# An mLSTM and mixer kernel: the weight decoding of the first batch moved back by one chunk

## The chip, the cores and the metric

The kernel runs on one core of a Trainium2 chip. The metric is the device time of one execution in microseconds (us). An execution's own time holds its span, which is what the profile shows, and a little around it.

## The reference

For four batches the kernel computes an mLSTM layer with 8 heads of 40 over 768 steps, and then a token and channel mixer with ReLU and residuals:

```python
for t in range(S):                      # mLSTM, kept stable by a running maximum m
    m_new = max(f_gate + m, i_gate)
    C = exp(f_gate + m - m_new) * C + exp(i_gate - m_new) * outer(v, k)
    n = exp(f_gate + m - m_new) * n + exp(i_gate - m_new) * k
    y = sigmoid(o_gate) * (C @ q) / max(abs(n @ q), 1)
x = y as [B, S, 320]
h = relu(x.T @ w_tok1) @ w_tok2         # over the tokens, 768 -> 256 -> 768
u = x + h.T
out = u + relu(u @ w_ch1) @ w_ch2       # over the channels, 320 -> 1536 -> 320
```

## The kernel before

**Work.** A batch's 768 steps are cut into NC = 6 chunks of 128. A chunk (a unit `(b, c)`) is done in matrix form: scores `ps_sc` from queries and keys (`st_s`, L313), times decays `dd` (L323), applied to the values into `po` (`st_pv`, L439) on top of the part from the state, which needs scaled queries `q3t` (`prep_q3`, L274 to L280; L378), and an update of the state (`st_state`, L386, L391, L395). `x0_ops` makes the chunk's output `x` from `po` (L476 to L485) and splits it into a high part `xh` on ScalarE (L490) and a low part `xl` (L491), since the mixer works with pairs of rounded fp32 numbers. The mixer over the tokens is `a_part` (matmuls `ps_a`, one row of products per chunk), `a_end` (Relu into `rh` on ScalarE, L711, and its low part `rl` on VectorE, L712), and `phase_b` (matmuls `ps_b` with `w2` from `rh` and `rl`). Both run through the helper `mm3`, L694. The mixer over the channels is `gemm1w` (L807) and `gemm2w`.

**Weights.** They come packed, in 30 pieces of 128 x 384: pieces 0 to 3 are `w1` (for ps_a), 4 to 7 `w2` (for ps_b), 8 and 9 the first of `c1`, 10 and 11 the first of `c2`, 12 and 13 `c1` again, and so on. A piece goes through five steps, in pairs:

- `dec_load` (L641): SyncE loads it into `wst`, up to the piece that the argument names.
- `dec_abs`: ScalarE makes `pf` in PSUM (L652, Prelu); then the lower bits are turned into integers in `wst`, by ScalarE (L656) or GpSimd (L658). While `early[0]` is set, ScalarE does this for every piece, and `pf` lies in the banks of `ps_acc`; later GpSimd does it for the even pieces, and `pf` lies in `ps_s`, unless a bank is named.
- `dec_ops`: VectorE joins both into `wf` (L670). This is a generator; each `step` runs one piece.
- `dec_hi`: ScalarE rounds `wf` into the high weights (L682).
- `dec_low`: GpSimd makes the low weights (L688).

**Order.** Each engine and the queue of SyncE serve their instructions in the order in which the program writes them; nothing is reordered. In the first batch a loop over c = 1 to 5 (L932 on) writes a turn: scores of the next chunk, its queries and keys, the state and output of this chunk, and the preparation of the chunk after. Into every turn it puts decoding. In turns 2 to 4 the two L670 of a pair stand between the halves of L323 (`mid=dg`) and behind the state update, in turn 1 both behind the state update. Behind the turn's output come `dec_hi`, `dec_low` and the next pair's `dec_abs`. In turn 4 pieces 8 and 9 are started in the middle, 10 at the end, and 11 at the end of turn 5. Behind the loop VectorE joins 8 and 9, TensorE finishes ps_a, and `rh`, `rl`, the transposes `gt` of the gates (L156, L158) and ps_b follow.

Of the kernel before, what the change touches and what calls it, by code (L numbers as in the profile page):

```python
# [19 lines left out]
NC = S // L  # L20
# [15 lines left out]
def kernel(ctx: ExitStack, tc: tile.TileContext, gates, qk, q3, kv, og,  # L36
# [7 lines left out]
    ps_acc = ctx.enter_context(tc.tile_pool(name="ps_acc", bufs=2, space=PSUM))  # L44
# [3 lines left out]
    def f32(x):  # L48
        return x.bitcast(F32)
# [175 lines left out]
    def load_qk(u, hf):  # L225
        b, c = u
        t = T.setdefault(u, {})
        if hf == 0:
            t["raw"] = raws[units.index(u) % 3]
        nc.sync.dma_start(out=t["raw"][64 * hf:64 * hf + D], in_=qk[b, c, hf])  # L230

    def load_phi(u):
        b, c = u
        T.setdefault(u, {})
        third = b < 2 and c % 3 == 2
        dd = ap.tile([128, H, L], F32, tag="p12" if third else "dd", name="dd", bufs=1 if third else 2)
        if b:
            nc.sync.dma_start(out=dd, in_=phi_d[c, b * HP:b * HP + H].partition_broadcast(128))
        T[u]["dd"] = dd

    def load_kv(u):
        b, c = u
        if b == 0 and c == 2:
            kvt = sp.tile([128, DM + H * E1], F32, tag="kv", name="kvt")
        else:
            kvt = ap.tile([128, DM + H * E1], F32, tag="kv", name="kvt")
        nc.sync.dma_start(out=kvt, in_=kv[b, c * L:(c + 1) * L, :])
        T[u]["kv"] = kvt
# [58 lines left out]
    def st_s(u, mult=True, mid=iter(()), rows=64, pool=(ps_s, "s")):  # L307
        t = T[u]
        t["s"] = [pool[0].tile([128, 4, L], F32, tag=pool[1], name="ps_sc") for _ in range(2)]
        for h in range(4):  # L310
            for hf in range(2):
                r = t["raw"][64 * hf:64 * hf + rows]
                nc.tensor.matmul(t["s"][hf][:, h, :], r[:, 1, h, :], r[:, 0, h, :], start=True, stop=True)  # L313
        if mult:
            st_p(u, mid)

    def st_p(u, mid=iter(())):
        t = T[u]
        for hf in range(2):
            if hf:  # L320
                next(mid, None)
            dd = t["dd"][:, 4 * hf:4 * hf + 4, :]
            nc.vector.tensor_tensor(dd, t["s"][hf], dd, ALU.mult)  # L323
# [148 lines left out]
    def x0_ops(u):  # L472
        b, c = u
        v = nc.vector
        po, n = T[u]["po"], T[u]["bank"][:, 400:400 + H]
        v.tensor_tensor(po[:, :, 0:D], po[:, :, 0:D],  # L476
                        sig[(b, c // 3)][:, c % 3, :].rearrange("p (h d) -> p h d", d=D), ALU.mult)
        yield
        den = ap.tile([128, H], F32, tag="den", name="den")
        v.tensor_scalar(den, po[:, :, D], 1.0, None, op0=ALU.max)  # L480
        v.scalar_tensor_tensor(n, po[:, :, D], -1.0, den, op0=ALU.mult, op1=ALU.max)
        v.reciprocal(den, n)
        yield
        x = ap.tile([128, DM], F32, tag="x", name="x", bufs=6)
        v.tensor_tensor(x.rearrange("p (h d) -> p h d", d=D), po[:, :, 0:D],  # L485
                        den.unsqueeze(2).to_broadcast([128, H, D]), ALU.mult)
        yield
        pool = xpool[2] if c in (3, 4) else sp
        xh, xl = (pool.tile([128, DM], F32R, tag=a, name=a, bufs=3 if pool is sp else 2) for a in ("xh", "xl"))
        nc.scalar.activation(xh, x, AF.Copy)  # L490
        (v if c == NC - 1 else nc.gpsimd).tensor_tensor(xl, x, f32(xh), ALU.subtract)  # L491
        xs[u] = (x, xh, xl)
        del T[u]
        yield
# [137 lines left out]
    nxt = [0, 0, 0]  # L632
    his, lows, wx, early = [], [], [], [True]

    def dec_load(n):
        while nxt[0] < min(n, len(pieces)):
            d, w, a = pieces[nxt[0]]
            k = nxt[0]
            pool, n_b = (xpool[2], 2) if k in (2, 3, 8, 9) else (wx[0], 3) if wx and (k - wx[1]) % 7 < 3 else (wq, 4)
            t = pool.tile([128, WP, 2], I32, tag="wst", name="wst", bufs=n_b)  # L640
            nc.sync.dma_start(out=t.rearrange("p n t -> p (n t)"), in_=w[:, a:a + WP].bitcast(I32))  # L641
            staged[nxt[0]] = t
            nxt[0] += 1
# [3 lines left out]
    def dec_abs(n, bank=None, both=False):  # L647
        while nxt[1] < min(n, len(pieces)):
            raw = staged[nxt[1]]
            pool, tag = bank or ((ps_acc, "acc") if early[0] else (ps_s, "s"))  # L650
            f = pool.tile([128, WP], F32, tag=tag, name="pf")
            nc.scalar.activation(f, raw[:, :, 1].bitcast(F32), AF.Prelu, scale=W_BIAS, alpha=W_SIGN)  # L652
            low = raw[:, :, 0]
            top16 = raw.rearrange("p n t -> p (n t)").bitcast(U16).rearrange("p (n t) -> p n t", t=4)[:, :, 1]
            if early[0] or nxt[1] % 2 and not both:
                nc.scalar.activation(low, top16, AF.Identity, scale=2.0 ** -13, bias=floor_b)  # L656
            else:
                nc.gpsimd.tensor_scalar(low, top16, 2.0 ** -13, 2.0 ** -14 - 0.5, op0=ALU.mult, op1=ALU.add)  # L658
            ready[nxt[1]] = (f, wq.tile([128, WP], F32, tag="wf", name="wf", bufs=4))
            nxt[1] += 1  # L660

    def dec_ops(more, m=2):
        n = nxt[2]
        if n >= len(pieces):
            return
        v = nc.vector
        ps = [(staged.pop(m),) + ready.pop(m) + pieces[m] for m in range(n, min(n + m, len(pieces)))]
        for p in ps:
            raw, f, w, *_ = p
            v.scalar_tensor_tensor(w.bitcast(I32), f.bitcast(I32), 3, raw[:, :, 0],  # L670
                                   op0=ALU.logical_shift_left, op1=ALU.bitwise_or)
            his.append(p)
            yield
        nxt[2] += len(ps)
        if more:
            dec_load(n + more)
        yield

    def dec_hi(n=2):
        for _ in range(min(n, len(his))):  # L680
            _, _, f, d, _, a = his.pop(0)
            nc.scalar.activation(d[0][:, a:a + WP], f, AF.Copy)  # L682
            lows.append((f, d, a))

    def dec_low(n=4):
        for _ in range(min(n, len(lows))):
            f, d, a = lows.pop(0)
            nc.gpsimd.tensor_tensor(d[1][:, a:a + WP], f, f32(d[0][:, a:a + WP]), ALU.subtract)  # L688
# [86 lines left out]
    acc = {}  # L775
# [71 lines left out]
    def step(g, n=1):  # L847
        for _ in range(n):
            next(g, None)
# [61 lines left out]
    x0 = x0_ops(u0)  # L911
# [18 lines left out]

    for c in range(1, NC):
        u, n1, n2, n3 = (units[c + i] for i in range(4))  # L932
        if c == 1:
            st_s(n1)
        elif c < NC - 1:
            dg = dec_ops(0)
            st_s(n1, mid=dg)
        if c < 3:
            load_phi(n3)
            load_qk(n3, 0)  # L940
            load_qk(n3, 1)
        if c == 1:
            dec_load(4)
        if c < NC - 1:
            spread_q(n1)
            prep_q3(n1)
            prep_kw(n1)
        if c == NC - 2:
            rows_w()
            early[0] = False  # L950
            dec_abs(nxt[1] + 2)
        if c == 1:
            dec_abs(2)
        st_state(u)
        if c == 1:
            dg = dec_ops(0)
        if c < NC - 1:
            step(dg, 2 if c == 1 else 9)
        st_pv(u)
        if c < 4:  # L960
            load_kv(n2)
            load_q3(n2)
        dec_load(2 * c + 4)
        x0 = x0_ops(u)
        step(x0, 2)
        if c == 2:
            nc.sync.dma_start(out=phi_d.rearrange("c r t -> r c t"), in_=phi.rearrange("p (c t) -> p c t", t=L))
        if c < 4:
            spread_split(n2)
            prep_exp(n2, 0)  # L970
            prep_exp(n2, 1)
        if c == NC - 2:
            a_part(0, 0, 0)
            a_part(0, 1, 0)
        if c < NC - 1:
            step(dg, 9)
            dec_hi()
            dec_low()
            if c == NC - 2:
                step(x0, 9)  # L980
                dec_abs(nxt[1] + 1, (ps_acc, "acc"))
            else:
                dec_abs(nxt[1] + 2)
        step(x0, 9)
        if c == NC - 1:
            dec_abs(nxt[1] + 1, (ps_acc, "acc"))
        if c > 3:
            load_sig(1, c - 4)
    ss = (ps_s, "s")
    dg = dec_ops(0)  # L990
# [9 lines left out]
    for b in range(B):  # L1000
# [35 lines left out]
        if b == 0:  # L1036
# [9 lines left out]
            dg = dec_ops(9)  # L1046
# [128 lines left out]
```

## Time and profile before

| | before |
|---|---|
| median of 3 runs | 426.87 us (426.71 to 427.46) |
| the profiled execution | 426.81 us, of which the span is 424.9 us |
| TensorE busy | 419.7 us (99%) |
| VectorE, ScalarE, GpSimd busy | 280.5, 184.0, 142.7 us |
| chain that ended last | TensorE 94% |
| granted TensorE clock in the span | 1.0 of full speed |

Times in the profile are microseconds from the start of the span. A busy TensorE is not TensorE at its peak, since its matmuls overlap; where an instruction starts, and for what it waited, is read from the timeline of its engine. In a timeline several equal instructions stand in one line (x2), with the time from the first's start to the last's end; neighbours on one engine overlap a little, so the distance from one start to the next is shorter than the duration.

### The profile page before, as it was taken

Reading aid. Unit: us, or ns where it says so; the run is one execution under the profiler, and the core shown is the slowest. Engines: PE = TensorE matmul, PEld = TensorE weight load, DVE = VectorE, ACT = ScalarE, POOL = GpSimd, SP = SyncE. Lnnn points to the kernel's source line nnn. Section 1 sums busy time; section 2 is a strip of 40 time slices with the busy share of each in tenths; the row PEclk is TensorE's granted clock in tenths of the full one; section 3 lists DMA queues with packets and bytes.
Section 4 is the critical chain, followed back from the end, with each engine's and each line's share of the span. In section 5 each row is a group of like instructions: output and inputs, shape, how many; then the busy total and the mean of one; then the engine's idle time right before and its main releaser. Section 6 shows DMA issues by size and latency. Waiting matters only on the chain.

```text
span 424.9 us, 8988 instructions
## 1 busy us (share of the span) xinstructions
PE 419.7 (99%) x3510; PEld 396.8 (93%) x3510; DVE 280.5 (66%) x620; ACT 184.0 (43%) x426; POOL 142.7 (34%) x186
## 2 busy tenths in 40 slices
PE   8999999999999999999999999999999999999996
PEld 4888989999999999999999999999999999988996
DVE  8988565515876788799696698789796647111412
ACT  5978569893455635234323346334144112111211
POOL 7488488751544501241341230331350110000000
PEclk9999999999999999999999999999999999999999
DMA  7997658941876713333346121533320000000000
GB/s 218 278 292 268 241 170 290 272 147 52 253 199 195 213 39 104 123 117 125 95 154 195 35 93 43 137 116 93 119 86 32 0 23 12 0 2 0 35 28 31
DMA packets 24574, 52.34 MB, mean 123 GB/s; under 512 B 2565, under 2 KB 13325, under 8 KB 24533
## 3 DMA queue, kind: packets, MB, share of 16 engines
q1 hardware_dynamic: 24293, 51.61, 39.4%
q8 instruction: 27, 0.44, 0.5%
q10 hardware_dynamic: 240, 0.18, 0.1%
q14 instruction: 14, 0.11, 0.1%
HBM read 47.73 MB, written 4.04 MB: 122 GB/s over the span
## 4 chain that ended last, share of the span: by engine, by line
PE 94%; ACT 2%; POOL 2%; issue 0%; DVE 0%; POOLq 0%
PE acc L694 30%; PE ps_h L788 22%; PE ps_h L807 11%; PE ps_b L694 5%; PE ps_sc L313 5%; PE ps_a L694 5%; PE po L439 4%; PE po L409 3%; PE pu L386 3%; PE po L415 2%; PE po L378 1%; PE warm L854 1%; ACT dd L291 1%; PE ps_t L762 1%; PE ps_t L760 1%; PE ps_t L761 1%
## 5 line engine op out<-in xcount | busy, mean ns | idle before, releaser
L788 PE MATMUL ps_h<-uT,c1h 128*128 128x256 f32 x480 | 93.4, 282 | 0.0
L694 PE MATMUL acc<-c2h,gh 128*128 128x320 f32 x288 | 89.2, 319 | 0.0
L793 ACT ACTIVATE gh<-ps_h 128x512 fp32r<-128x512 f32 x48 | 28.7, 597 | 135.4 <-PE ps_h L788 132.4
L694 PE MATMUL acc<-c2l,gh 128*128 128x320 f32 x288 | 86.4, 309 | 0.0
L788 PEld LDWEIGHTS ps_h<-uT,c1h 128*128 128x128 f32 x480 | 76.9, 188 | 0.5
L788 PE MATMUL ps_h<-uT,c1l 128*128 128x256 f32 x288 | 74.3, 280 | 0.0
L794 DVE SCALAR_TENSOR_TENSOR gl<-ps_h,gh 128x512 fp32r<-128x512 f32 x48 | 33.0, 688 | 45.4 <-ACT gh L793 45.3
L694 PE MATMUL acc<-c2h,gl 128*128 128x320 f32 x288 | 61.8, 308 | 0.0
L694 PEld LDWEIGHTS acc<-c2h,gh 128*128 128x128 f32 x288 | 54.1, 188 | 1.6
L694 PEld LDWEIGHTS acc<-c2l,gh 128*128 128x128 f32 x288 | 54.2, 188 | 0.9
L788 PEld LDWEIGHTS ps_h<-uT,c1l 128*128 128x128 f32 x288 | 54.3, 188 | 0.0
L811 DVE SCALAR_TENSOR_TENSOR gl<-ps_h,gh 128x512 fp32r<-128x512 f32 x24 | 16.6, 692 | 49.0 <-ACT gh L810 49.0
L458 POOL TENSOR_TENSOR sig<-sig,ht 128x320 f32<-128x320 f32 x18 | 14.7, 816 | 98.4 <-DVE ht L419 90.0
L294 ACT ACTIVATE dd<-dd,bcol 128x128 f32<-128x128 f32 x144 | 45.8, 392 | 4.5 <-POOL dd L284 4.3
L694 PEld LDWEIGHTS acc<-c2h,gl 128*128 128x128 f32 x288 | 47.2, 188 | 0.0
L807 PE MATMUL ps_h<-uT,c1h 128*128 128x512 f32 x120 | 36.0, 394 | 0.0
L323 DVE TENSOR_TENSOR dd<-ps_sc,dd 128x512 f32<-128x512 f32 x48 | 30.9, 681 | 3.3 <-PE ps_sc L313 3.3
L509 POOL TENSOR_TENSOR xl<-x,xh 128x320 fp32r<-128x320 f32 x18 | 15.8, 877 | 51.1 <-DVE xh L507 46.3
L810 ACT ACTIVATE gh<-ps_h 128x512 fp32r<-128x512 f32 x24 | 14.3, 594 | 41.2 <-PE ps_h L807 41.2
L313 PE MATMUL ps_sc<-raw 64*128 64x128 f32 (+1 forms) x384 | 26.8, 282 | 0.0
L313 PEld LDWEIGHTS ps_sc<-raw 64*128 64x128 f32 (+1 forms) x384 | 23.1, 187 | 3.3 <-issue 1.7
L807 PEld LDWEIGHTS ps_h<-uT,c1h 128*128 128x128 f32 x120 | 22.1, 188 | 3.9
(152 smaller groups left out, 858.3 us busy)
## 6 DMA issues: line engine op xcount, KB each, us to landing
dd<-phi_d SPq DMA_DIRECT2D x18, 512.0 KB
wst<-in_wc_dram SPq DMA_DIRECT2D x22, 384.0 KB
kvt<-in_kv_dram SPq DMA_DIRECT2D x24, 324.0 KB
raw<-in_qk_dram SPq DMA_DIRECT2D x48, 160.0 KB
sig<-in_og_dram SPq DMA_DIRECT2D x8, 480.0 KB
out_dram<-x SPq DMA_DIRECT2D x24, 160.0 KB
q3t<-in_q_dram SPq DMA_DIRECT2D x20, 180.0 KB
wst<-in_wt_dram SPq DMA_DIRECT2D x8, 384.0 KB
```

Source lines behind the costliest of these rows:

```text
L294: nc.scalar.activation(dd[:, h, :], dd[:, h, :], AF.Exp, bias=bcol[:, c, HP * b + h:HP * b + h + 1])
L313: nc.tensor.matmul(t["s"][hf][:, h, :], r[:, 1, h, :], r[:, 0, h, :], start=True, stop=True)
L323: nc.vector.tensor_tensor(dd, t["s"][hf], dd, ALU.mult)
L439: nc.tensor.matmul(o, t["dd"][:, ROW[h], :], x, start=c == 0 and h == 0, stop=h == H - 1)
L458: nc.gpsimd.tensor_tensor(sg, sg, ht[:, :, 0:D], ALU.mult)
L509: nc.gpsimd.tensor_tensor(xl, x, f32(xh), ALU.subtract)
L694: nc.tensor.matmul(ps, a, m, start=(first and i == 0), stop=(last and i == n - 1))
L788: nc.tensor.matmul(ps[:, j, :], c1[x][:, a:a + 128], u[:, y, :], start=part is first and i == 0 and (order == 0 or j == 0), stop=i == len( ...
L793: nc.scalar.activation(gh, ps, AF.Relu)
L794: nc.vector.scalar_tensor_tensor(gl, ps, 0.0, f32(gh), op0=ALU.max, op1=ALU.subtract)
L807: nc.tensor.matmul(ps, c1[x][:, a:a + 128], u[:, :, y, :], start=n == 0, stop=n == len(todo) - 1)
L811: nc.vector.scalar_tensor_tensor(gl, ps, 0.0, f32(gh), op0=ALU.max, op1=ALU.subtract)
```

## The change

No pair is decoded by VectorE in turn 1. Turns 2 to 5 decode the pairs 0/1, 2/3, 4/5 and 6/7, where turns 1 to 4 did. The loads, the first step and the high and low copies move with them. Pieces 8 to 11, which were started in the middle of turn 4 (8, 9), at its end (10) and at the end of turn 5 (11), are all started at the end of turn 5. `early[0]` is cleared there, too. The loads of 12 and 13 move out of the loop to the call behind it. What TensorE does, and in which order, stays the same.

```diff
@@ -930,37 +930,26 @@
 
     for c in range(1, NC):
         u, n1, n2, n3 = (units[c + i] for i in range(4))
-        if c == 1:
-            st_s(n1)
-        elif c < NC - 1:
-            dg = dec_ops(0)
+        dg = dec_ops(0) if c > 1 else iter(())
+        if c < NC - 1:
             st_s(n1, mid=dg)
         if c < 3:
             load_phi(n3)
             load_qk(n3, 0)
             load_qk(n3, 1)
-        if c == 1:
-            dec_load(4)
         if c < NC - 1:
             spread_q(n1)
             prep_q3(n1)
             prep_kw(n1)
         if c == NC - 2:
             rows_w()
-            early[0] = False
-            dec_abs(nxt[1] + 2)
-        if c == 1:
-            dec_abs(2)
         st_state(u)
-        if c == 1:
-            dg = dec_ops(0)
-        if c < NC - 1:
-            step(dg, 2 if c == 1 else 9)
+        step(dg, 9)
         st_pv(u)
         if c < 4:
             load_kv(n2)
             load_q3(n2)
-        dec_load(2 * c + 4)
+        dec_load(2 * c + 2)
         x0 = x0_ops(u)
         step(x0, 2)
         if c == 2:
@@ -972,18 +961,15 @@
         if c == NC - 2:
             a_part(0, 0, 0)
             a_part(0, 1, 0)
-        if c < NC - 1:
-            step(dg, 9)
-            dec_hi()
-            dec_low()
-            if c == NC - 2:
-                step(x0, 9)
-                dec_abs(nxt[1] + 1, (ps_acc, "acc"))
-            else:
-                dec_abs(nxt[1] + 2)
+        if c == NC - 1:
+            step(x0, 9)
+            early[0] = False
+        dec_hi()
+        dec_low()
+        dec_abs(2 * c)
+        if c == NC - 1:
+            dec_abs(nxt[1] + 2, (ps_acc, "acc"))
         step(x0, 9)
-        if c == NC - 1:
-            dec_abs(nxt[1] + 1, (ps_acc, "acc"))
         if c > 3:
             load_sig(1, c - 4)
     ss = (ps_s, "s")
```

**ScalarE, from the scaled queries of chunk 5 to the first `rh`.** Before, with `xh_739` and `xh_772` the outputs of chunks 4 and 5, `wf_653` and `wf_657` pieces 6 and 7, and `wst_621`, `wst_623`, `wst_716`, `wst_718` pieces 8 to 11:

```order
L274 ACTIVATE pq_620<-ps_q_677 120x384
L652 ACTIVATE pf_685<-wst_621 128x384
L652 ACTIVATE pf_689<-wst_623 128x384
L656 ACTIVATE wst_623<-wst_623,floor_b_133 128x384
L682 ACTIVATE w2h_143<-wf_653 128x384
L682 ACTIVATE w2h_143<-wf_657 128x384
L490 ACTIVATE xh_739<-x_737 128x320
L652 ACTIVATE pf_743<-wst_716 128x384
L490 ACTIVATE xh_772<-x_770 128x320
L652 ACTIVATE pf_776<-wst_718 128x384
L656 ACTIVATE wst_718<-wst_718,floor_b_133 128x384
L711 ACTIVATE rh_811<-ps_a_725 128x320
```

After, from the outputs of chunks 4 and 5 (`xh_721`, `xh_752`) on; `wf_714` and `wf_718` are pieces 6 and 7, `wst_690`, `wst_692`, `wst_741` and `wst_743` pieces 8 to 11:

```order
L490 ACTIVATE xh_721<-x_719 128x320
L490 ACTIVATE xh_752<-x_750 128x320
L682 ACTIVATE w2h_143<-wf_714 128x384
L682 ACTIVATE w2h_143<-wf_718 128x384
L652 ACTIVATE pf_760<-wst_690 128x384
L652 ACTIVATE pf_764<-wst_692 128x384
L656 ACTIVATE wst_692<-wst_692,floor_b_133 128x384
L652 ACTIVATE pf_768<-wst_741 128x384
L652 ACTIVATE pf_772<-wst_743 128x384
L656 ACTIVATE wst_743<-wst_743,floor_b_133 128x384
L711 ACTIVATE rh_807<-ps_a_699 128x320
L711 ACTIVATE rh_807<-ps_a_703 128x320
```

Two high copies, four L652 and two L656 now stand between the output of chunk 5 and `rh`; before it were one L652 and one L656.

**VectorE, from the second L670 of turn 4 to the first step of chunk 5's output.** Before, `po_693` is chunk 4, `po_749` chunk 5, and `wf_657` piece 7:

```order
L670 SCALAR_TENSOR_TENSOR wf_657<-pf_654,wst_525 128x384
L476 TENSOR_TENSOR po_693<-po_693,sig_173 128x8x40
L480 TENSOR_SCALAR den_721<-po_693 128x8
L481 SCALAR_TENSOR_TENSOR po_693<-po_693,den_721 128x8
L482 RECIPROCAL den_721<-po_693 128x8
L485 TENSOR_TENSOR x_737<-po_693,den_721 128x320
L476 TENSOR_TENSOR po_749<-po_749,sig_173 128x8x40
```

After, `po_667` is chunk 4, `po_727` chunk 5, `wf_639` piece 5, and `wf_714` and `wf_718` are pieces 6 and 7:

```order
L670 SCALAR_TENSOR_TENSOR wf_639<-pf_636,wst_507 128x384
L476 TENSOR_TENSOR po_667<-po_667,sig_173 128x8x40
L480 TENSOR_SCALAR den_695<-po_667 128x8
L481 SCALAR_TENSOR_TENSOR po_667<-po_667,den_695 128x8
L482 RECIPROCAL den_695<-po_667 128x8
L485 TENSOR_TENSOR x_719<-po_667,den_695 128x320
L670 SCALAR_TENSOR_TENSOR wf_714<-pf_711,wst_603 128x384
L670 SCALAR_TENSOR_TENSOR wf_718<-pf_715,wst_605 128x384
L476 TENSOR_TENSOR po_727<-po_727,sig_173 128x8x40
```

The pair 6/7 has moved from turn 4 to the place ahead of chunk 5's output.

**GpSimd, from the scaled queries of chunk 5 on.** Before, with pieces 6 and 7 as `wf_653` and `wf_657`, and 8 and 10 as `wst_621` and `wst_716`:

```order
L280 TENSOR_TENSOR q3t_618<-q3t_618,pq_620 120x384
L149 TENSOR_TENSOR w_row_683<-z_100 36x640
L658 TENSOR_SCALAR wst_621<-wst_621 128x384
L688 TENSOR_TENSOR w2l_144<-wf_653,w2h_143 128x384
L688 TENSOR_TENSOR w2l_144<-wf_657,w2h_143 128x384
L491 TENSOR_TENSOR xl_740<-x_737,xh_739 128x320
L658 TENSOR_SCALAR wst_716<-wst_716 128x384
```

After, with pieces 4 to 7 as `wf_635`, `wf_639`, `wf_714`, `wf_718`, and 8 and 10 as `wst_690` and `wst_741`:

```order
L280 TENSOR_TENSOR q3t_600<-q3t_600,pq_602 120x384
L149 TENSOR_TENSOR w_row_665<-z_100 36x640
L688 TENSOR_TENSOR w2l_144<-wf_635,w2h_143 128x384
L688 TENSOR_TENSOR w2l_144<-wf_639,w2h_143 128x384
L491 TENSOR_TENSOR xl_722<-x_719,xh_721 128x320
L688 TENSOR_TENSOR w2l_144<-wf_714,w2h_143 128x384
L688 TENSOR_TENSOR w2l_144<-wf_718,w2h_143 128x384
L658 TENSOR_SCALAR wst_690<-wst_690 128x384
L658 TENSOR_SCALAR wst_741<-wst_741 128x384
```

The integers of piece 8 have moved from a place ahead of all these low copies to one behind them.

## Rows read from the trace of the kernel before

**Rows 1.** Waits of TensorE, whole execution: us in total, times, longest.
```profile
PE warm L854 <- POOL zero L61: 1.4, 1, 1.4
PE po L378 <- POOL q3t L280: 0.3, 1, 0.3
```

**Rows 2.** Windows: stretch, its us, busy (x) per engine, clock, DMA share, GB/s.
```profile
1.00:3.00 2.00, 1.61 (x4) 0.59 (x5) 1.38 (x2) 0.79 (x1) 1.76 (x7) 1.00 0.41 121
...
17.47:23.77 6.30, 6.23 (x63) 5.32 (x62) 6.08 (x17) 4.48 (x12) 5.92 (x8) 1.00 0.99 279
23.77:29.70 5.93, 5.93 (x62) 5.19 (x62) 4.76 (x13) 4.90 (x12) 5.29 (x7) 1.00 0.96 307
...
49.40:56.30 6.90, 6.90 (x50) 6.74 (x50) 4.87 (x12) 4.33 (x14) 3.70 (x7) 1.00 0.77 236
56.30:70.00 13.70, 13.70 (x74) 12.07 (x74) 7.38 (x14) 10.05 (x24) 11.55 (x16) 1.00 0.61 200
```

**Rows 3.** Timeline, ScalarE, turns 4 and 5: start, us, instruction [idle before].
```profile
37.06 0.52 ACT L652 ACTIVATE pf<-wst 128x384 f32<-128x384 f32 x1
37.52 0.64 ACT L656 ACTIVATE wst<-wst,floor_b 128x384 int32<-128x384 uint16 x1
38.05 0.52 ACT L652 ACTIVATE pf<-wst 128x384 f32<-128x384 f32 x1
...
39.39 0.47 ACT L274 ACTIVATE pq<-ps_q 120x384 f32<-120x384 f32 x1
40.17 0.52 ACT L652 ACTIVATE pf<-wst 128x384 f32<-128x384 f32 x1 [0.31 <-DMA wst<-in_wc_dram]
41.21 0.52 ACT L652 ACTIVATE pf<-wst 128x384 f32<-128x384 f32 x1 [0.52 <-DMA wst<-in_wc_dram]
...
42.20 0.93 ACT L682 ACTIVATE w2h<-wf 128x384 fp32r<-128x384 f32 x2
43.02 0.46 ACT L490 ACTIVATE xh<-x 128x320 fp32r<-128x320 f32 x1
...
46.01 0.47 ACT L490 ACTIVATE xh<-x 128x320 fp32r<-128x320 f32 x1 [2.11 <-DVE x L485]
46.39 0.52 ACT L652 ACTIVATE pf<-wst 128x384 f32<-128x384 f32 x1
46.83 0.64 ACT L656 ACTIVATE wst<-wst,floor_b 128x384 int32<-128x384 uint16 x1
48.24 0.87 ACT L711 ACTIVATE rh<-ps_a 128x320 fp32r<-128x320 f32 x2 [0.77 <-PE ps_a L694]
```

**Rows 4.** Timeline, TensorE, the start of `ps_b`.
```profile
49.38 0.41 PE L694 MATMUL ps_b<-rh,w2h 128*128 128x320 f32 x1
...
50.07 0.45 PE L694 MATMUL ps_b<-rl,w2h 128*128 128x320 f32 x2
```

**Rows 5.** Timeline, VectorE, turns 1, 4, 5 and the handover.
```profile
22.08 1.01 DVE L670 SCALAR_TENSOR_TENSOR wf<-pf,wst 128x384 int32<-128x384 int32 x2
...
40.84 0.55 DVE L670 SCALAR_TENSOR_TENSOR wf<-pf,wst 128x384 int32<-128x384 int32 x1
...
44.24 0.50 DVE L476 TENSOR_TENSOR po<-po,sig 128x320 f32<-128x320 f32 x1 [1.27 <-PE po L439]
...
48.72 0.93 DVE L712 SCALAR_TENSOR_TENSOR rl<-ps_a,rh 128x320 fp32r<-128x320 f32 x2 [0.67 <-ACT rh L711]
```

**Rows 6.** Timeline, SyncE, the loads of weight pieces (several in a row merged).
```profile
35.35 1.96 SPq L641 DMA_DIRECT2D wst<-in_wc_dram  x4
...
49.16 25.53 SPq L641 DMA_DIRECT2D wst<-in_wc_dram  x16
```

**Rows 7.** Timeline, ScalarE, the decoding of pieces 12 and 13.
```profile
58.82 0.94 ACT L652 ACTIVATE pf<-wst 128x384 f32<-128x384 f32 x2
```

**Rows 8.** Timeline, GpSimd, turn 5.
```profile
43.33 1.97 POOL L688 TENSOR_TENSOR w2l<-wf,w2h 128x384 fp32r<-128x384 f32 x2
...
46.23 0.54 POOL L658 TENSOR_SCALAR wst<-wst 128x384 int32<-128x384 uint16 x1
```

## The prediction

> **What bounds the kernel now.** I read four views. The waits first: in the whole execution TensorE shows two waits, 1.4 us for its first operand and 0.3 us for the scaled queries of chunk 5 [rows 1]. So whatever holds TensorE up is added to the end, and nothing else counts. The windows next: a turn of the chunk loop takes 6.30 us (turn 1) or 5.93 us (turn 2), and TensorE is busy for 6.23 and 5.93 of them; the MLP's first stretch, 49.40 to 56.30, and the one behind it have no idle time at all, all at a granted clock of 1.00, which is 2.4 GHz [rows 2]. A delay that reaches TensorE before 49.4 us therefore has no slack to vanish in. Then the timelines of ScalarE, VectorE and GpSimd between 37 and 50 us, where the change lands, and of TensorE at the handover from token mixing part one (`ps_a`) to part two (`ps_b`).
>
> The handover is the place to look at. ps_b needs `rh`, ScalarE's Relu of ps_a. ScalarE is free for it: it idles 0.77 us until ps_a is done and starts at 48.24 [rows 3]. TensorE meanwhile runs the gate transposes `gt` and starts ps_b at 49.38 [rows 4]; rh's first half was ready at 48.24 + 0.44 = 48.68. So before the change rh has 0.7 us to spare.
>
> **The change part by part.** *What goes from the early turns.* Turn 1 loses two L670 instructions of VectorE (1.01 us for the pair [rows 5]), and the weight work of ScalarE and GpSimd slides back by a turn. Does TensorE get anything for it? Turn 2 runs at 5.93 us, all of it TensorE's own work, with its pair in place, so a pair per turn is hidden by the turn's matmuls [rows 2]. Turn 1 is 0.37 us longer, 6.30 - 5.93; that is the most that can be gained there. I take 0: the missing pair stood behind the work that TensorE needed in turn 1, and TensorE's idle time is only 6.30 - 6.23 = 0.07 us. For the 0.3 us wait in turn 5 [rows 1] the scaled queries hang on ScalarE's `pq` at 39.39, behind two hi copies and two pieces of decoding of turn 3. After the change turn 3 has exactly as many, of pieces two lower. Bounds 0 and -0.31; I take 0.
>
> *Turn 4.* ScalarE no longer starts pieces 8 and 9 after pq, where it waited 0.31 and 0.52 us for their loads [rows 3]. It now does hi of 4 and 5, then decodes 6 and 7. Hi of 5 waits for VectorE's second L670 of the turn, 40.84 + 0.55 = 41.39 [rows 5]. From there by start-to-start distances [rows 3]: a hi copy 0.41 (42.20 to 43.02 is two), L652 to L656 0.46 (37.06 to 37.52), L656 to L652 0.53 (37.52 to 38.05). So L652 of 6 starts at about 41.87, L656 of 6 at 42.33, L652 of 7 at 42.86, L656 of 7 at 43.32, and that ends at 43.32 + 0.64 = 43.96. Their loads go out where those of 8 and 9 did (SyncE's four at 35.35 [rows 6]) and landed then by 40.17 and 41.21, so they are there in time.
>
> *Turn 5, VectorE.* L670 of pieces 6 and 7 now stands ahead of chunk 5's L476. The second waits for L656 of 7: 44.00 to 44.55, and L476, which started at 44.24 [rows 5], starts about 0.47 after it, at 44.47 (0.47 is the distance in a pair, 1.01 - 0.54): **+0.23 us**. `xh` of chunk 5 follows on ScalarE, 46.01 + 0.23 = 46.24. Of ps_a's products, which TensorE ends at about 48.2, only the last need it, more than a microsecond later, so this costs TensorE nothing by itself.
>
> *Turn 5, ScalarE: the term that matters.* Between xh of chunk 5 and rh there were one L652 and one L656: 46.39 to about 47.4, then idle until 48.24. Now there stand two hi copies, four L652 and two L656. Distances: xh to the next 0.38 (46.01 to 46.39); hi copies 0.82; L652 to L652 0.42 (a pair busy 0.94 us with one at 0.52 [rows 7]) twice; L652 to L656 0.46 twice; L656 to the next 0.53 twice. Sum 0.38 + 0.82 + 2 x (0.42 + 0.46 + 0.53) = 4.02 us. rh's first half starts at 46.24 + 4.02 = 50.26 in place of 48.24: **2.02 us late**. It ends at 50.70, the second at 48.24 + 0.87 + 2.02 = 51.13.
>
> The Trainium skill, "ScalarE: Activation LUTs", section "What ACT_TABLE_LOAD costs", gives an ACTIVATE a fixed part and 0.833 ns per element, more with a per-partition bias, and lets neighbours overlap by about 93 ns. For 384 elements that is an estimate of 0.413 us from start to start (0.506 with the bias of L656), so 0.82 + 4 x 0.413 + 2 x 0.506 = 3.49 us for the eight, against 3.64 by the rows, and the delay of TensorE below would be 0.15 us less. The hi copies agree with it; the decoding steps are slower in the rows, so the sum keeps the rows.
>
> *GpSimd and VectorE beside it.* GpSimd's lows of 6 and 7 wait for their hi copies (46.62 on): from about 47.2, two for 1.97 us [rows 8], to 49.15; then L658 of piece 8, 0.54 us [rows 8], to 49.7. VectorE's L670 of 8 and 9 wait for that and stand ahead of `rl`: 49.8 to about 50.8. rl of the first half can start at 50.7 to 50.8, when rh is there anyway. A tie; it costs 0, at worst some 0.3 us.
>
> *TensorE.* The first ps_b product waits for rh, 50.70 + 0.05 = 50.75 against 49.38: +1.37. The two rl products then wait for rl, which ended 0.54 us after rh (48.72 + 0.93 = 49.65 against 49.11 [rows 3, 5]): 51.13 + 0.54 = 51.67, so the second goes at about 51.70 against 50.07 + 0.15 = 50.22 [rows 4]: **+1.48 us**. Behind it everything is released by TensorE's own products in the old order, and TensorE had no idle time to make it up. I put the delay at 1.5 us. Bounds: +1.1, if turn 1's 0.37 is gained, and +0.8, if the 0.31 of turn 5 is gained as well; +2.0, if rh's whole lateness and VectorE's tie count.
>
> *Loads.* Pieces 12 and 13 went out inside the loop; they now stand behind the release of the early pool, where SyncE went on at 49.16 [rows 6], with 14, 15 and 16. Five pieces of 393 kB at the 236 GB/s of that stretch [rows 2] take 8.3 us, to about 57.5. Piece 12 is decoded at 58.82 [rows 7], and by the delay 1.5 us later. Nothing waits: 0. If this cover went, TensorE would wait for c1's third piece.
>
> The profiled execution took 426.81 us (span 424.9); the median of the runs is 426.87, so the two agree to 0.06. 426.87 + 1.5 = **428.4 us**.
>
> **The rivals.** *The relief counts too* (0.10): turn 1 falls to 5.93 us and the wait for the queries goes, so all of turn 5 starts 0.68 us sooner, and of the 1.5 only 0.8 is left: 427.7. For it speaks that VectorE was busy 6.08 of 6.30 us in turn 1 [rows 2]; against it, that TensorE was busy too.
>
> *Faster* (0.04): the same 0.68 us is gained and rh is not late. The point from which this decides is ScalarE's queue at xh of chunk 5: it idled 2.11 us before it [rows 3]; were the hi copies and L652 of 8 and 9 done in that hole (about 2.1 us), rh would start near 48.2. Time 426.2. Against it stands the order of the change: all eight are behind xh, on a queue that is served in order.
>
> *A longer tail* (0.05): GpSimd's lows or the burst of five loads make VectorE's L670 of 8 later by a microsecond, and rl with it: 429.4. Against: the tie above and the 2 us between landing and use.
>
> *The clock* (0.03): TensorE stands idle for about 1.4 us at 49.4, which it does nowhere in the middle of this trace, and falls to 1.2 GHz. If the stretch 49.40 to 56.30, dense with matmuls, ran at half rate, that would be 6.9 us more: 435.3. Against it: it had idled 1.4 us at the start, too [rows 1], and the two microseconds behind that were granted 1.00 [rows 2]. The Trainium skill, "TensorE: Matmul & The Clock Gate", section "Why this matters for your kernels", has the rule that pauses between bursts of matmuls can throw the clock back to the half rate; by that rule this change could cost several times what I forecast. No row here shows a fall, so it gets little.
>
> **How the numbers follow.** The forecast case, rh late on ScalarE's queue and 1.1 to 2.0 us added, has 0.78. A measurement of this kernel can tell about 0.2% from no change, that is 0.85 us. Slower by more than that: 0.78 + 0.05 + 0.03 = 0.86. Within: 0.10, the relief case at +0.8. Faster: 0.04. The range reaches from 427.4, which takes in most of the relief case, to 429.3, which is the top of the forecast case and part of the longer tail.
>
> **What would show it.** In the profile of the changed kernel ScalarE runs eight weight instructions between the two last `xh` copies' end and rh, with no idle time before rh (0.77 us before), and rh starts near 50.3. TensorE idles 1.2 to 1.5 us in front of ps_b, put down to ScalarE's rh, and a little at the rl products. Turns 1 and 2 stay at 6.30 and 5.93 us. The stretches behind 56 us are the same, 1.5 us later. I am wrong if rh starts before 49.4, if the first ps_b product waits for something else (GpSimd's low of piece 6, say), if turn 1 gets shorter, or if a TensorE stretch behind is shorter than before and gives the delay back.

## The result, and the profile after

The changed kernel takes 429.32 us (median of 6 executions, 428.23 to 430.45) against 426.82 us (6 executions, 426.68 to 427.46): a ratio of 1.0053, 95% interval 1.0042 to 1.0065, that is 1.8 to 2.8 us slower. Six executions spread over 2.2 us, where the kernel before spreads over 0.8. They fall into two kinds, told apart by the granted TensorE clock of the whole span:

| execution | span, us | granted clock |
|---|---|---|
| 1, 2, 6 of the changed kernel | 428.2, 428.3, 427.9 | 0.996, 0.995, 0.996 |
| 3, 4, 5 of the changed kernel | 427.1, 426.5, 426.6 | 0.999, 1.0, 0.999 |
| the profiled one before | 424.9 | 1.0 |

At the full clock the span is 1.6 to 2.2 us longer than the profiled one before; at 0.995 or 0.996 it is 3.0 to 3.4 us longer. Part of the scatter is the kernel's own: in 36 later executions the kernel before has spans of 424.6 to 426.2 us. The profiled execution of the changed kernel is one of the second kind (430.17 us, span 428.2).

TensorE's waits, whole execution (total, times, longest), which answer to [rows 1]:

```profile
PE ps_b L694 <- ACT rh L711: 1.3, 1, 1.3
PE ps_sc L313 <- DMA raw<-in_qk_dram: 0.8, 1, 0.8
PE ps_phi L180 <- DVE z L175: 0.6, 1, 0.6
PE po L378 <- POOL q3t L280: 0.3, 1, 0.3
```

The one that the change brings is the first: TensorE waits 1.3 us for ScalarE's `rh`. The wait for the queries of chunk 5 is as long as before. The two between them lie ahead of 13 us, and so ahead of anything that the change moves; of them 0.25 us was left when the gate transposes began (48.83 against 48.58).

ScalarE's timeline (start, us, instruction, idle time before it), which answers to [rows 3]:

```profile
46.48 0.47 ACT L490 ACTIVATE xh<-x 128x320 fp32r<-128x320 f32 x1 [1.97 <-DVE x L485]
46.86 0.93 ACT L682 ACTIVATE w2h<-wf 128x384 fp32r<-128x384 f32 x2
47.69 0.93 ACT L652 ACTIVATE pf<-wst 128x384 f32<-128x384 f32 x2
48.56 0.64 ACT L656 ACTIVATE wst<-wst,floor_b 128x384 int32<-128x384 uint16 x1
49.11 0.95 ACT L652 ACTIVATE pf<-wst 128x384 f32<-128x384 f32 x2
49.99 0.64 ACT L656 ACTIVATE wst<-wst,floor_b 128x384 int32<-128x384 uint16 x1
50.53 0.73 ACT L711 ACTIVATE rh<-ps_a 128x320 fp32r<-128x320 f32 x2
```

From the `xh` at 46.48 on it is busy without a gap: two hi copies, two L652, an L656, two L652, an L656, and only then rh, at 50.53 in place of 48.24. VectorE, which answers to [rows 5]:

```profile
44.72 0.49 DVE L476 TENSOR_TENSOR po<-po,sig 128x320 f32<-128x320 f32 x1
...
50.08 1.02 DVE L670 SCALAR_TENSOR_TENSOR wf<-pf,wst 128x384 int32<-128x384 int32 x2 [2.60 <-ACT pf L652]
51.01 0.88 DVE L712 SCALAR_TENSOR_TENSOR rl<-ps_a,rh 128x320 fp32r<-128x320 f32 x2
```

The joins of 8 and 9 end at 51.1, and `rl` starts at 51.01, just when rh is there. The profile puts the wait of the joins down to ScalarE's L652, but what ended last before them is GpSimd's conversion of piece 8, which stands behind its lows of 6 and 7 (the first of the two L658, near 50.06). GpSimd, to [rows 8]:

```profile
47.45 1.98 POOL L688 TENSOR_TENSOR w2l<-wf,w2h 128x384 fp32r<-128x384 f32 x2 [1.80 <-ACT w2h L682]
49.51 1.14 POOL L658 TENSOR_SCALAR wst<-wst 128x384 int32<-128x384 uint16 x2
```

TensorE, to [rows 4]:

```profile
49.16 0.54 PE L158 MATMUL gt<-id_t,z 36*128 36x36 f32 x6
50.99 0.41 PE L694 MATMUL ps_b<-rh,w2h 128*128 128x320 f32 x1 [1.29 <-ACT rh L711]
...
51.71 0.65 PE L694 MATMUL ps_b<-rl,w2h 128*128 128x320 f32 x2
...
53.40 0.47 PE L694 MATMUL ps_b<-rh,w2h 128*128 128x320 f32 x1
...
56.15 0.31 PE L694 MATMUL ps_b<-rh,w2h 128*128 128x320 f32 x1
```

`gt` ends at 49.70, ps_b starts at 50.99. The last two lines show the other half of the loss: at 53.40 one product of 320 columns lasts 0.47 us, at 56.15 the same product 0.31. The windows, to [rows 2] (stretch, its us, busy (x) per engine, clock, DMA share, GB/s):

```profile
48.60:51.00 2.40, 1.11 (x15) 0.80 (x13) 0.93 (x2) 2.40 (x7) 1.89 (x3) 1.00 0.28 45
51.00:58.00 7.00, 7.00 (x37) 6.75 (x38) 3.90 (x10) 3.21 (x11) 2.11 (x5) 0.76 0.89 323
58.00:72.00 14.00, 14.00 (x79) 12.41 (x78) 7.90 (x16) 10.07 (x23) 11.84 (x16) 1.00 0.55 162
```

The stretch behind 58 us is dense, as before; from 51 to 58 us the granted clock is 0.76. In finer windows:

```profile
52.00:52.50 0.50, 0.50 (x5) 0.50 (x5) 0.10 (x1) 0.00 (x0) 0.00 (x0) 1.00 1.04 412
52.50:53.00 0.50, 0.50 (x5) 0.50 (x4) 0.39 (x1) 0.00 (x0) 0.00 (x0) 0.68 1.01 406
53.00:53.50 0.50, 0.50 (x4) 0.50 (x3) 0.00 (x0) 0.26 (x1) 0.15 (x1) 0.50 0.99 399
...
55.50:56.00 0.50, 0.50 (x4) 0.50 (x3) 0.23 (x1) 0.24 (x2) 0.41 (x1) 0.50 1.19 399
56.00:56.50 0.50, 0.50 (x5) 0.50 (x4) 0.00 (x0) 0.40 (x2) 0.32 (x1) 0.91 0.98 283
```

The clock is still full for 1.5 us behind the pause, falls to 0.50 (1.2 GHz) during the half microsecond from 52.5, stays there, and is back by 56.5. The first product of the channel mixer, before and after:

```profile
56.26 0.40 PE L807 MATMUL ps_h<-uT,c1h 128*128 128x512 f32 x1
```
```profile
59.65 0.40 PE L807 MATMUL ps_h<-uT,c1h 128*128 128x512 f32 x1
```

From the first ps_b product to this one TensorE took 59.65 - 50.99 = 8.66 us, where it had taken 56.26 - 49.38 = 6.88: 1.78 us more. Of these, 0.23 is lost at the first two rl products, which end 1.37 us behind the first ps_b product (51.71 + 0.65) in place of 1.14 (50.07 + 0.45, [rows 4]), still at full clock. The other 1.55 us is the clock.

### The profile page after: what moved, and what is told of

It is laid out like the page before. It is cut to its first block, busy times and chain, and to the rows that moved or that the text cites. A ratio compares the mean times of both kernels' runs of the same rounds, so it can differ in the third digit from the quotient of the medians.

```text
span 428.2 us, 8984 instructions
## 1 busy us (share of the span) xinstructions
PE 420.2 (98%) x3509; PEld 398.1 (93%) x3510; DVE 279.2 (65%) x620; ACT 183.4 (43%) x426; POOL 142.2 (33%) x186
## 4 chain that ended last, share of the span: by engine, by line
PE 93%; DMA 2%; ACT 2%; DVE 1%; issue 0%; ACTq 0%; DVEq 0%; SPq 0%
PE acc L694 30%; PE ps_h L788 21%; PE ps_h L807 10%; PE ps_b L694 5%; PE ps_sc L313 5%; PE po L439 4%; PE ps_a L694 4%; PE po L409 3%; PE pu L386 3%; PE po L415 2%; DMA raw<-in_qk_dram 1%; PE po L378 1%; DMA i_t<-in_gates_dram 1%; ACT wst L656 1%; PE ps_t L760 1%; PE ps_t L762 1%
## 5 line engine op out<-in xcount | busy, mean ns | idle before, releaser
L694 PE MATMUL acc<-c2h,gh 128*128 128x320 f32 x288 | 89.2, 319 | 0.0
L694 PE MATMUL acc<-c2l,gh 128*128 128x320 f32 x288 | 86.4, 309 | 0.0
L694 PE MATMUL acc<-c2h,gl 128*128 128x320 f32 x288 | 61.8, 308 | 0.0
L694 PEld LDWEIGHTS acc<-c2h,gh 128*128 128x128 f32 x288 | 54.1, 188 | 1.6
L694 PEld LDWEIGHTS acc<-c2l,gh 128*128 128x128 f32 x288 | 54.2, 188 | 0.9
L694 PEld LDWEIGHTS acc<-c2h,gl 128*128 128x128 f32 x288 | 47.2, 188 | 0.0
```

The costliest lines, as they stand in the source:

```text
L694: nc.tensor.matmul(ps, a, m, start=(first and i == 0), stop=(last and i == n - 1))
```

## The experiments

Two questions were open. Is ScalarE's queue the only thing that makes ps_b late, or is VectorE's rl late by itself, as the tie in the prediction says it might be? And does the clock fall because of the pause?

**e1: ScalarE's part taken back, GpSimd's left.** The conversion of piece 8 on GpSimd is kept for later:

```diff
         dec_low()
-        dec_abs(2 * c)
         if c == NC - 1:
-            dec_abs(nxt[1] + 2, (ps_acc, "acc"))
+            for g in wait:
+                g()
+            dec_abs(12, (ps_acc, "acc"))
+        else:
+            dec_abs(2 * c)
         step(x0, 9)
+        if c == NC - 2:
+            early[0] = False
+            wait = []
+            dec_abs(10, put_off=wait)
```

The rest of the edit, left out here, makes `dec_abs` put GpSimd's instruction into `wait`, and drops `early[0] = False` from turn 5. It shifts line numbers by 5 (L699 for L694, L717 for L712).

> ScalarE's two L652 and one L656 of pieces 8 and 9 go to the end of turn 4, where ScalarE idles for 2 us; GpSimd's L658 of piece 8 stays behind the lows of 6 and 7. Theory 'two paths': rh starts 1.4 us earlier, near 49.1, ps_b near 49.7, but VectorE still holds rl until the joins of 8 and 9 are done near 51.0, so TensorE waits about 1.2 us in front of the first rl product in place of 1.3 in front of the first ps_b product, and at full clock the time stays at 428.0 to 428.3. Rival 'ScalarE's queue alone': the delay shrinks to 0.1 to 0.4 us, 426.9 to 427.3.

Measured: 428.44 us (427.94 to 429.87, 6 executions), ratio to before 1.004, interval 1.0027 to 1.0054. TensorE's wait, ScalarE's rh and VectorE's joins and rl:

```profile
PE ps_b L699 <- DVE rl L717: 1.1, 1, 1.1
```
```profile
48.74 0.73 ACT L716 ACTIVATE rh<-ps_a 128x320 fp32r<-128x320 f32 x2
```
```profile
49.71 1.02 DVE L675 SCALAR_TENSOR_TENSOR wf<-pf,wst 128x384 int32<-128x384 int32 x2 [2.61 <-POOL wst L658]
50.64 0.88 DVE L717 SCALAR_TENSOR_TENSOR rl<-ps_a,rh 128x320 fp32r<-128x320 f32 x2
```

rh starts at 48.74, 1.8 us sooner than in the changed kernel (1.4, less the 0.4 by which this execution was ahead at the gate transposes), and TensorE starts ps_b at 49.25 without a wait. It then stops behind its four rh products until 51.18, in front of the first rl product: VectorE is held by the joins of 8 and 9, and these by GpSimd's conversion behind the lows of 6 and 7. The wait has only changed its name. At full clock (five of the six) the median is 428.42 us, where the three of the changed kernel have 428.27: nothing is gained; what sets the two medians of all executions apart is how many of them lost the clock. "ScalarE's queue alone" is refuted.

**e2: GpSimd's part taken back, ScalarE's left.** The conversion of piece 8 goes ahead of the lows:

```diff
         dec_hi()
+        if c == NC - 1:
+            dec_abs(2 * c)
         dec_low()
```

> Only GpSimd's L658 of piece 8 goes ahead of the lows of 6 and 7; ScalarE's queue is as in the changed kernel. Both theories: VectorE's joins of 8 and 9 are done near 49.8, rh stays near 50.5, TensorE waits 1.3 us for it; 428.0 to 428.3 at full clock, 0.2 us at most below the changed kernel. If instead the GpSimd path were the only one, 426.9 to 427.3.

Measured: 428.38 us (427.82 to 430.06, 6 executions), ratio 1.0045, interval 1.003 to 1.006.

```profile
PE ps_b L694 <- ACT rh L711: 1.3, 1, 1.3
```
```profile
47.80 0.56 DVE L670 SCALAR_TENSOR_TENSOR wf<-pf,wst 128x384 int32<-128x384 int32 x1 [0.79 <-ACT pf L652]
48.76 0.56 DVE L670 SCALAR_TENSOR_TENSOR wf<-pf,wst 128x384 int32<-128x384 int32 x1 [0.40 <-ACT wst L656]
50.48 0.89 DVE L712 SCALAR_TENSOR_TENSOR rl<-ps_a,rh 128x320 fp32r<-128x320 f32 x2 [1.16 <-ACT rh L711]
```

VectorE is done with the joins at 49.3 and then idles 1.16 us for rh. At full clock (four of the six) the median is 428.28 us, the same as the changed kernel's 428.27. So each of the two paths is enough to hold TensorE up by itself, and taking away one of them gains next to nothing.

**e3: both taken back.** Pieces 8 and 9 are started as a whole at the end of turn 4; the pairs of L670, and the hi copies and lows of 6 and 7, stay where the change has put them:

```diff
-            early[0] = False
         dec_hi()
         dec_low()
-        dec_abs(2 * c)
         if c == NC - 1:
-            dec_abs(nxt[1] + 2, (ps_acc, "acc"))
+            dec_abs(12, (ps_acc, "acc"))
+        else:
+            dec_abs(2 * c)
         step(x0, 9)
+        if c == NC - 2:
+            early[0] = False
+            dec_abs(10)
```

> Pieces 8 and 9 are started as a whole at the end of turn 4: both paths get shorter. Theory 'two paths': rh near 49.1, rl behind it at once, no wait of TensorE over 0.3 us at the handover, 426.8 to 427.3, granted clock 1.00 in every execution, and a spread under 0.5 us as before. Rival 'the moved pairs themselves cost something elsewhere': 427.5 or more.

Measured: 427.13 us (426.67 to 428.06, 11 executions), ratio 1.0004, interval 0.9995 to 1.0013. ScalarE's rh; VectorE's joins and rl; TensorE's last gt, first ps_b and first rl products:

```profile
49.10 0.73 ACT L711 ACTIVATE rh<-ps_a 128x320 fp32r<-128x320 f32 x2
```
```profile
47.37 1.02 DVE L670 SCALAR_TENSOR_TENSOR wf<-pf,wst 128x384 int32<-128x384 int32 x2
49.54 0.89 DVE L712 SCALAR_TENSOR_TENSOR rl<-ps_a,rh 128x320 fp32r<-128x320 f32 x2 [1.15 <-ACT rh L711]
```
```profile
49.13 0.54 PE L158 MATMUL gt<-id_t,z 36*128 36x36 f32 x6
49.60 0.41 PE L694 MATMUL ps_b<-rh,w2h 128*128 128x320 f32 x1
...
50.28 0.62 PE L694 MATMUL ps_b<-rl,w2h 128*128 128x320 f32 x2
```

No wait of TensorE for rh or rl is left that its list of waits would show, and the clock is 0.999 to 1.0 in all 11 executions. The first two rl products still take 0.62 us in place of 0.45 [rows 4], so some 0.2 us may be left. So the moved pairs themselves cost nothing that these times can tell from zero (-0.2 to 0.6 us by the interval); what costs is that 8 and 9 are started behind them. The spread was not under 0.5 us, as expected, but 1.4; the kernel before had 1.2 in the same hour.

**e4: the pause filled.** Five dummy matmuls on a tile of zeros, between ps_a and gt:

```diff
+            warm(5)
             cols()
```

> The changed kernel with five dummy matmuls of 0.22 us between ps_a and the gate transposes, so that TensorE works through most of the time in which it waits for rh. Theory 'the clock falls because of the pause': granted clock 1.00 in every execution, 428.1 to 428.5 in all of them, the spread of 2.2 us is gone. Rival 'the lower clock is a disturbance of its own': the clock stays below 1 in about half of the executions and the times spread from 428.2 to 430.4. If the dummy matmuls lay on the path, 429.3 at full clock.

Measured: 429.06 us (428.71 to 429.55, 5 executions), ratio 1.0049, interval 1.0037 to 1.0061. The clock is 0.999 to 1.0 in all five, and the spread is 0.8 us.

```profile
48.80 1.25 PE L854 MATMUL warm<-zero 128*128 128x512 bf16 x5
...
51.05 0.42 PE L694 MATMUL ps_b<-rh,w2h 128*128 128x320 f32 x1 [0.20 <-ACT rh L711]
```

TensorE still starts ps_b at about 51, and the 0.47 us products are gone. The level was missed: the median is 0.6 us above the top of what was expected, and not far below the 429.3 of the case with the dummies on the path. In the profiled execution (span 426.7) they were not on it, since TensorE still waited 0.20 us for rh behind them. The other four have spans of 427.0 to 427.4, against 426.5 to 427.1 of the changed kernel at full clock; they were not profiled, and where the rest comes from stays open.

**e5: a late rh and nothing else.** The kernel before, with ScalarE copying a table of constants onto itself six times ahead of rh:

```diff
     step(dg, 2)
+    for _ in range(6):
+        nc.scalar.activation(bm_t, bm_t, AF.Copy)
```

> The kernel before, with six dummy Copy instructions on ScalarE (a table of constants onto itself) ahead of rh; every piece of weights is decoded where it was. Theory 'a late rh is all that counts': rh near 50.5, TensorE waits 1.2 to 1.6 us for it, 428.2 to 428.8 at full clock, as the changed kernel. Theory 'the pause costs the clock': in about a third of the executions the granted clock is near 0.995 and the time 1.6 us higher. Rival 'the clock fell because of something in the moved decoding': clock 1.00 in all of them.

Measured: 429.96 us (428.28 to 431.17, 8 executions), ratio 1.006, interval 1.0041 to 1.0079. Three executions at 0.999 take 428.28 to 428.85 us, about what was expected of a late rh (spans of 426.4 to 427.0); five at 0.995 or 0.996 have spans of 427.7 to 429.4. ScalarE, TensorE's first ps_b product and the windows of the profiled execution, which is one of the five:

```profile
47.23 3.23 ACT L993 ACTIVATE bm_t<-bm_t 120x369 f32<-120x369 f32 x6
50.37 0.75 ACT L711 ACTIVATE rh<-ps_a 128x320 fp32r<-128x320 f32 x2
```
```profile
50.84 0.64 PE L694 MATMUL ps_b<-rh,w2h 128*128 128x320 f32 x1 [1.53 <-ACT rh L711]
```
```profile
50.00:50.50 0.50, 0.00 (x0) 0.00 (x0) 0.00 (x0) 0.50 (x2) 0.00 (x0) 1.00 1.01 111
50.50:50.75 0.25, 0.00 (x0) 0.00 (x0) 0.00 (x0) 0.25 (x2) 0.00 (x0) 0.52 0.39 86
...
51.00:52.00 1.00, 1.00 (x4) 1.00 (x5) 0.70 (x2) 0.61 (x3) 0.00 (x0) 0.50 1.01 396
...
53.00:54.00 1.00, 1.00 (x6) 1.00 (x5) 0.34 (x1) 0.26 (x1) 0.24 (x1) 0.54 0.55 218
54.00:55.00 1.00, 1.00 (x9) 0.99 (x8) 0.71 (x2) 0.19 (x2) 0.09 (x1) 1.00 0.00 0
```

With the decoding untouched, a rh that is 2.1 us late does what the change does, in both halves: the pause, and the clock at 0.50. Here it is at 0.50 when the first product starts. The share of executions was five of eight, more than the third that was expected.

**e6: the same, filled** (e5 with the dummy matmuls of e4).

> The same with five dummy matmuls between ps_a and the gate transposes. Both clock theories: granted clock 1.00 in every execution. The wait of TensorE for rh shrinks to 0.2 to 0.5 us, but rh is as late, so 428.2 to 428.9 in all executions.

Measured: 429.12 us (428.69 to 429.72, 6 executions), ratio 1.0043, interval 1.0029 to 1.0056. The clock is 0.999 or 1.0 in all six, and TensorE waits 0.4 us for rh in the profiled one. The median is 0.2 us above the top of the expectation.

**e7: one part of the change alone.** In the kernel before, pieces 8 to 11 are started at the end of turn 5; the pairs stay in turns 1 to 4 (the comments are added here):

```diff
-            dec_abs(nxt[1] + 2)                      # turn 4, middle
...
-                dec_abs(nxt[1] + 1, (ps_acc, "acc")) # turn 4, end
...
-            dec_abs(nxt[1] + 1, (ps_acc, "acc"))     # turn 5, end
+            dec_abs(nxt[1] + 2)
+            dec_abs(nxt[1] + 2, (ps_acc, "acc"))
```

> The kernel before with one part of the change alone: pieces 8 to 11 are all started at the end of turn 5, the pairs of turns 1 to 4 stay. Between xh of chunk 5 and rh stand four L652 and two L656, no hi copies: rh at 46.0 + 0.4 + 2.8 = 49.2, 1.0 us later than before, ps_b at 49.7 (+0.3), the second rl product at about 50.7 (+0.45). So 427.2 to 427.5: of the delay of 1.5 us the late starts make a third, and the moved pair 6/7 the rest. If the starts were all of it: 428.3.

Measured: 427.56 us (426.92 to 428.54, 12 executions), ratio 1.0007, interval 0.9996 to 1.0017, the clock 0.999 or 1.0 in all twelve.

```profile
46.44 0.47 ACT L490 ACTIVATE xh<-x 128x320 fp32r<-128x320 f32 x1 [2.53 <-DVE x L485]
...
49.65 0.73 ACT L711 ACTIVATE rh<-ps_a 128x320 fp32r<-128x320 f32 x2
```
```profile
50.12 0.41 PE L694 MATMUL ps_b<-rh,w2h 128*128 128x320 f32 x1 [0.24 <-ACT rh L711]
```

rh comes 3.21 us behind `xh` of chunk 5 (4.05 in the changed kernel, 2.23 before), and TensorE waits 0.24 us. It is 0.3 us by the ratio, with an interval that still holds no change; the trace shows that the wait is there: against its gate transposes ps_b starts 0.3 us later than before (0.78 us behind the last of them in place of 0.47), and the rl products lose another 0.2, together the third of the delay that was expected. The late starts alone are nearly hidden. It takes the hi copies and lows of pair 6/7 ahead of them to make the pause long.

**e8: a longer pause.** The changed kernel with three more copies of the table ahead of rh.

> The changed kernel with three dummy Copy instructions on ScalarE ahead of rh, so that TensorE waits about 1.5 us longer. rh's lateness goes to the end one to one: 429.6 to 430.2 at full clock. Theory 'the pause costs the clock': the share of executions with a clock of about 0.995 rises above a third, and they take 1.6 us or more on top. Rival 'a disturbance of its own': the share stays or is zero.

Measured: 432.05 us (431.31 to 432.49, 5 executions), ratio 1.0107, interval 1.009 to 1.0124.

```profile
PE ps_b L694 <- ACT rh L711: 2.8, 1, 2.8
```

TensorE's wait is 1.5 us longer than in the changed kernel, as expected. All five executions have a clock of 0.992 to 0.996. None is left at full clock, so the 429.6 to 430.2 can't be compared directly. The profiled one (432.49 us) lost about 1.55 us to the clock, by the same reading as above, and its gate transposes began 1.0 us later than those of the kernel before; without both it would come to 429.9. Two of the others have 0.992, more than one such stretch accounts for, and were not profiled. Over all kernels, the wait being that of the one profiled execution of each:

| wait at the handover, from the profile | kernels | executions with a clock of 0.996 or less |
|---|---|---|
| 0.4 us or less | e3, e4, e6, e7 and the kernel before | none of 34, and none of 36 |
| 1.1 to 1.3 us | e1, e2, changed kernel | 1 of 6, 2 of 6, 3 of 6 |
| 1.5 us | e5 | 5 of 8 |
| 2.8 us | e8 | 5 of 5 |

The longer TensorE stands idle there, the oftener the clock falls: never in 70 executions up to 0.4 us, in 6 of 18 at 1.1 to 1.3 us, in 10 of 13 above. The steps between 1.1 and 1.3 us are too few executions to order. "A disturbance of its own" and "something in the moved decoding" are both refuted.

## Why the prediction was right, and where it was short

- **TensorE has no slack** held: every delay at the handover went to the end. From the first product of the channel mixer to the end of the span it is 368.5 to 369.1 us in all ten profiles, whatever happened before.
- **The relief of turn 1 counts 0** held, for another reason than the one given. From scores to scores turn 1 takes 6.14 us in e1, where the pair is gone, and 6.15 in e5, where it is there (6.12 to 6.65 over e1 to e4 and e8, 6.13 to 6.30 in e5 to e7 and before). In each of them TensorE stops for some 0.2 us behind `ps_phi`'s first product until GpSimd is done with its split of the gates (L175, to 22.52 before); VectorE's pair has no part in it. The 0.07 us of idle time that the prediction read off the windows is too little: the next `ps_phi` product comes 0.45 us behind the first there (22.12 and 22.57) and 0.21 in turn 2 (28.29 and 28.50). In the changed kernel's own profile the turn has 5.94 us, which the prediction had named as a sign against it; but it began 0.6 us late there, so that the split was done, and it ended 0.25 us later than before, not sooner. Turn 2 takes 5.93 us, as before (24.02 to 29.95), and e3, which keeps the relief, is no faster than the kernel before.
- **ScalarE's queue** held to a few hundredths. rh was forecast 4.02 us behind `xh` of chunk 5 and came 50.53 - 46.48 = 4.05 us behind it. Less the 0.25 us by which this execution was late from the start, rh starts at 50.28 (forecast 50.26) and ps_b at 50.74 (50.75).
- **VectorE's +0.23** held: L476 at 44.72, less 0.25, is 44.47, the forecast. (ps_a ends at 48.65 before, and not at about 48.2 as the prediction has it; nothing hangs on it.)
- **GpSimd and VectorE, a tie** held in time (joins done at 51.1 less 0.25, forecast 50.8), but its weight was not seen: priced at 0 to 0.3 us beside ScalarE's 1.4, it is a second path of the same length, as e1 shows. Whoever had mended ScalarE's queue by the prediction alone would have gained nothing.
- **Loads at 0** held: TensorE shows no wait for weights behind the handover.
- **The sum**, +1.5 us, fits the executions at full clock: 428.23, 428.27 and 429.06 us against 426.82. In the profiled one ps_b is 1.36 us late (forecast 1.37), and with the 0.23 at the rl products the delay ahead of the clock's fall is 1.59 us (forecast 1.48).
- **The clock** is where it was short. As a rival it was given 0.03 and 6.9 us; it came in three of six executions, and in the profiled one it costs 1.55 us, since TensorE ran at 1.2 GHz for some 3.4 us and not for the whole stretch. The medians of the two kinds' spans, 428.2 and 426.6, are 1.6 us apart as well. That is what lifts the median from 428.27 at full clock to 429.32. That the median still lies at the top of the range, which reaches so far for a later rh and a longer tail, is luck: it is the mean of 429.06 and 429.58, one of either kind, and a seventh execution would have moved it to one of them. The argument against the clock was weak: that it was full behind the 1.4 us of idle time at the start of the span says nothing of a pause in the middle. The rule of the Trainium skill ("TensorE: Matmul & The Clock Gate", section "Why this matters for your kernels"), that pauses between bursts of matmuls can send the clock back to the half rate, was the better guide. The trace agrees with its direction, 1.00 before the pause and 0.50 behind it; but the rule speaks of longer pauses than this one, and here the runs decide.

## What to carry to other kernels

Where two engines hand a tile to TensorE one after the other, put nothing that can wait in front of either on its queue: here the decoding of weights that were wanted 9 us later stood ahead of rh on ScalarE and of rl on VectorE, and each alone made TensorE wait 1.1 to 1.3 us. When such a wait is mended and the time does not move, look for the second path of the same length before giving the theory up. And price a pause of a busy TensorE higher than its length: here a wait of 1.3 us went with a loss of 1.6 us, or of 3.1 where the clock fell.

## What was not expected of the hardware

In the changed kernel the clock did not fall in the pause but more than 1.5 us behind its end, when TensorE was busy again (1.00 from 52.00 to 52.50, 0.50 from 53.00); in e5 it fell inside the pause, 0.3 us ahead of the first product (0.52 from 50.50 to 50.75, the product at 50.84). The same kernel shows the fall in some executions and not in others, and the share was higher behind longer pauses: 6 of 18 at 1.1 to 1.3 us, 5 of 8 at 1.5, 5 of 5 at 2.8. Between 1.1 and 1.5 us of idle time five to eight executions are hardly enough to see what a version costs: a median of the changed kernel could have come out anywhere between 428.3 and 430.2.

ScalarE's copies of a table onto itself came 0.52 us apart (rh starts 3.14 us behind the first of six), where the two hi copies, of about the same size, came 0.42 apart (46.86 to 47.69 for both). Each copy of the table reads what the one before wrote, and the hi copies do not depend on each other; that this is the reason was not tested.
